# Moving first copies, one ReLU, two squares and one softmax scaling to other engines or later slots in a TensorE-bound kernel

## The chip, the cores and the metric

The kernel runs on one core of one Trainium2 chip. The metric is the device time of one execution in microseconds, lower is better. A ratio below is the mean time of one kernel's fast executions over the mean of the other's in the same rounds, so it is not quite the ratio of the medians that stand beside it.

Engine names in the profile: PE is TensorE (matmul), PEld its weight load, ACT ScalarE, DVE VectorE, POOL GpSimd, SP the engine that only issues DMA (SyncE).

## The reference, cut to what matters

A dynamic convolution over time (7 taps, weights by a softmax per position and head) feeds a feed-forward layer with a squared ReLU.

```python
w = exp(weight_gen - max); w = w / (sum(w) + 1e-09)          # 8 x 4096 x 8 heads x 7 taps
x = einsum('bshk,bskhg->bshg', w, x_unf)                      # causal window of 7
h = np.maximum(x.reshape(32768, 192) @ w_in, 0.0)             # 192 -> 2048
out = (h * h @ w_out).astype(np.float32)                      # 2048 -> 192
```

## The kernel before

Tokens go in blocks: two of 512, then blocks of 1024. A *block* j is: bands (VectorE spreads softmax weights over a mask), `st_conv` (the convolution as banded matmuls into PSUM, then a copy to `y`), *units* `u` (12 or 6 matmuls into a PSUM tile `h`; ReLU on ScalarE to `t`; square on VectorE to `g`), and *output groups* `M` (half of the 2048 rows of `g` times `w_out`). The output groups of a block run while the next block's units run.

```python
ps_h = ctx.enter_context(tc.tile_pool(name="ps_h", bufs=3, space=bass.MemoryType.PSUM))
ps_o = ctx.enter_context(tc.tile_pool(name="ps_o", bufs=1, space=bass.MemoryType.PSUM))
...
def st_conv(j):
    ...                                   # matmuls into the tiles yps (tag "h": the same 3 buffers)
    for n, yp in enumerate(yps):
        k0, k1 = n * per, min((n + 1) * per, NK)
        nc.scalar.copy(out=y[:, k0:k1, 0:th],
                       in_=yp[:, 0 : (k1 - k0) * th].rearrange("p (k c) -> p k c", c=th))

def st_unit(j, u):
    ...                                   # 12 (or 6) matmuls into h
    nc.scalar.activation(out=t1, in_=h, func=ActF.Relu)
    nc.vector.tensor_tensor(out=g, in0=t1, in1=t1, op=AluOp.mult)
```

The order on every engine is the order of the program, and a string per block spells it: `E` exponential (ScalarE), `S` sum, reciprocal and scaling of a softmax piece (VectorE), after the last piece of a part the row moves (DMA, alternately issued by SP and GpSimd), `B` bands, `C` the next block's convolution followed by an x load issued by GpSimd, `X` a cast of x on VectorE, `L` the load of a softmax part (DMA, issued by SP), `u` a unit, `M` an output group. A digit is the number of the part or block.

```python
plans = {
    0: "B1 X1 u u u E1 S1 u C u u u u",
    1: "L3 u u B2 M E2 B3 u M E2 u u S2 u M u C u S2 M",
    ...
    3: "L5 L6 M S3 u u u M u u u u M u M B6 E4 u u u M M B7 u u S4 u E4 M u C M u",
}
```

The first `M` of block 1 (M1 below) reads units 0 to 3 of block 0, the second (M2) reads units 4 to 7, unit 4 first.

The softmax here doesn't subtract the row's maximum and nothing guards it: scores larger than these inputs give would overflow.

## Time and profile before

| | before |
|---|---|
| median, 4 executions | 747.93 us (747.69 to 749.93) |
| profiled span | 746.6 us, granted clock 1.000 |
| busy | TensorE 99%, ScalarE 84%, VectorE 83%, GpSimd 12% |
| chain that ended last | TensorE 94% |

The prediction shows the lines and reads them.

### The profile page before, as it was taken

The page shows a single profiled execution, that of the slowest core. Times are in us where ns is not written, and L with a number is a line of the kernel's source. Part 1 is how long each engine was busy: PE and PEld are TensorE (multiplying, and loading weights), DVE is VectorE, ACT ScalarE, POOL GpSimd, SP SyncE. Part 2 cuts the span into 40 slices and gives each one's busy share as a digit, 9 for nine tenths or more (in the row PEclk, how much of TensorE's full clock was granted, in tenths as well). Part 3 has the DMA queues.
Part 4 walks back from the last instruction along what each step waited for, and adds up shares of the span by engine and source line. Part 5 has one row for each costly group of instructions (what it writes and reads, how often), then busy time and mean ns, then how long its engine had stood idle before and what let it go on. Part 6 is the DMA issues. An engine that isn't in the chain of part 4 may idle for free.

```text
span 746.6 us, 33289 instructions
## 1 busy us (share of the span) xinstructions
PE 739.0 (99%) x15106; PEld 556.5 (75%) x15106; DVE 621.8 (83%) x1001; ACT 624.7 (84%) x755; POOL 88.8 (12%) x130
## 2 busy tenths in 40 slices
PE   8999999999999999999999999999999999999998
PEld 4767877877777777777777777787777777777787
DVE  5999998998889888888889888898888987677853
ACT  5998788888888888888888888888888888888874
POOL 7321220101101100011000110001100011001000
PEclk9999999999999999999999999999999999999999
DMA  8654454436554234644245542365441354441312
GB/s 223 112 106 109 80 101 85 100 70 139 94 118 79 75 57 80 140 79 73 45 74 139 102 65 53 51 139 108 59 80 48 57 108 80 60 73 51 51 46 65
DMA packets 122169, 64.81 MB, mean 87 GB/s; under 512 B 83849, under 2 KB 118636, under 8 KB 121516
## 3 DMA queue, kind: packets, MB, share of 16 engines
q1 hardware_dynamic: 77708, 45.66, 22.4%
q0 software_dynamic: 44176, 16.93, 20.5%
q8 instruction: 118, 1.93, 1.1%
q14 instruction: 23, 0.19, 0.1%
q10 hardware_dynamic: 144, 0.10, 0.0%
HBM read 48.61 MB, written 28.70 MB: 104 GB/s over the span
## 4 chain that ended last, share of the span: by engine, by line
PE 94%; DVE 2%; issue 1%; DMA 1%; ACT 1%; POOL 0%; DVEq 0%; ACTq 0%
PE o L475 45%; PE h L441 43%; PE yp L416 6%; DVE g L453 1%; DVE bd L348 1%; DMA wr<-v_first 0%; DMA wg<-in_weight_gen_dram 0%; POOL wr L330 0%; ACT t L450 0%; DVE v_first L239 0%; ACT ex L217 0%; DVE ssum L224 0%; DVE rcp L231 0%; DVE o_sb L491 0%; ACT y L427 0%
## 5 line engine op out<-in xcount | busy, mean ns | idle before, releaser
L450 ACT ACTIVATE t<-h 128x1024 f16<-128x1024 f32 x512 | 496.7, 1026 | 65.6 <-PE h L441 65.3
L453 DVE TENSOR_TENSOR g<-t 128x1024 f16<-128x1024 f16 x512 | 334.3, 687 | 100.5 <-ACT t L450 97.8
L475 PEld LDWEIGHTS <-g 64*128 64x128 f16 (+1 forms) x8032 | 352.3, 94 | 55.0 <-issue 4.8
L475 PE MATMUL o<-w_o,g 64*128 64x192 f16 (+1 forms) x8032 | 385.3, 243 | 0.9 <-DVE o_sb L491 0.6
L441 PE MATMUL h<-y,w_i 64*128 64x512 f16 (+1 forms) x3168 | 379.7, 370 | 2.2 <-ACT t L450 0.9
L441 PEld LDWEIGHTS <-w_i 64*128 64x128 f16 x3168 | 162.6, 94 | 117.2 <-issue 5.2
L348 DVE TENSOR_TENSOR bd<-wr,mask 128x4160 f16<-128x4160 f16 (+3 forms) x89 | 149.3, 1701 | 4.0 <-DMA wr<-v_first 4.0
L300 POOL DMA_DIRECT2D xt<-in_x_dram x62 | 51.2, 830 | 446.7 <-PE yp L416 423.7
L489 ACT COPY o_sb<-o 128x384 f32<-128x384 f32 x129 | 62.2, 482 | 33.8 <-PE o L475 33.8
L491 DVE TENSOR_TENSOR o_sb<-o,o_sb 128x384 f32<-128x384 f32 x123 | 68.2, 555 | 8.4 <-ACT o_sb L489 5.6
L427 ACT CAST y<-yp 128x1024 f16<-128x1024 f32 (+1 forms) x64 | 48.1, 803 | 14.5 <-PE yp L416 14.5
L416 PE MATMUL yp<-bd,xt 128*32 128x104 f16 (+8 forms) x3864 | 51.7, 208 | 0.3 <-DVE bd L348 0.2
L416 PEld LDWEIGHTS <-xt 128*32 128x32 f16 (+3 forms) x3864 | 46.2, 92 | 6.7 <-issue 6.2
L239 DVE TENSOR_TENSOR v_big<-ex,rcp 128x112 f16<-128x112 f32 (+1 forms) x136 | 27.3, 263 | 1.8 <-DMA vd<-v_big 0.6
L217 ACT ACTIVATE ex<-wg 128x448 f32<-128x448 f32 (+2 forms) x44 | 27.2, 618 | 1.8 <-DMA wg<-in_weight_gen_dram 1.8
L224 DVE TENSOR_REDUCE ssum<-ex 128x64 f32<-128x448 f32 (+2 forms) x44 | 26.1, 594 | 2.5 <-ACT ex L217 2.3
L231 DVE RECIPROCAL rcp<-ssum 128x64 f32<-128x64 f32 (+2 forms) x44 | 23.7, 539 | 1.5
L290 POOL DMA_DIRECT2D xt<-in_x_dram x7 | 3.8, 549 | 135.8 <-PE yp L416 135.8
L330 POOL DMA_DIRECT2D wr<-v_first x31 | 16.8, 561 | 16.3 <-DVE v_first L239 16.1
L539 PE MATMUL wp<-warm 128*128 128x512 f16 x39 | 11.4, 459 | 1.3 <-DVE warm L531 1.3
L539 PEld LDWEIGHTS <-warm 128*128 128x128 f16 x39 | 4.3, 114 | 7.6 <-issue 3.5
L239 DVE TENSOR_TENSOR v_first<-ex,rcp 128x112 f16<-128x112 f32 (+1 forms) x48 | 9.1, 255 | 0.3
(24 smaller groups left out, 28.2 us busy)
## 6 DMA issues: line engine op xcount, KB each, us to landing
out_dram<-o_sb SPq DMA_DIRECT2D x63, 384.0 KB, 3.0
xt<-in_x_dram POOLq DMA_DIRECT2D x42, 240.0 KB, 5.9
wg<-in_weight_gen_dram SPq DMA_DIRECT2D x4, 1064.0 KB, 8.3
xt<-in_x_dram POOLq DMA_DIRECT2D x20, 192.0 KB, 5.6
wr<-vd SPq DMA_DIRECT2D x38, 80.0 KB, 3.6
vd<-v_big SPq DMA_DIRECT2D x5, 512.0 KB, 5.5
wg<-in_weight_gen_dram SPq DMA_DIRECT2D x5, 392.0 KB
wg<-in_weight_gen_dram SPq DMA_DIRECT2D x3, 616.0 KB, 4.1
```

Of the source, the lines that this page charges most:

```text
L217: nc.scalar.activation(out=self.ex[:, lo:hi].rearrange("p r g k e -> p (r g) k e"), in_=self.wg[:, lo:hi].rearrange("p r (g e) k -> p (r g ...
L239: eng.tensor_tensor(out=bass.AP(tensor=v.tensor, offset=v.offset + lo * H * SL + lo % SL * 2 + g * SL * 2, ap=[list(v.ap[0]), [H * SL + 2, ...
L300: eng.dma_start(out=dst[:, first:last], in_=ap)
L348: nc.vector.tensor_tensor(out=bd_t[j][:, H * lo : H * (lo + len(tiles) * n)].rearrange("p (g m c) -> p g m c", g=shape[1], c=2 * SL), in0= ...
L416: nc.tensor.matmul(out=yps[k // per][p0 : p0 + m, col + a : col + b], lhsT=x_t[s][:, i, 32 * q : 32 * q + m], rhs=bd[:, h // 2, h % 2, a - ...
L427: nc.scalar.copy(out=y[:, k0:k1, 0:th], in_=yp[:, 0 : (k1 - k0) * th].rearrange("p (k c) -> p k c", c=th),)
L441: nc.tensor.matmul(out=h[:, half, jj * th : (jj + 1) * th], lhsT=w_in_chunk(u * per + jj, slot, half), rhs=y_t[j][r0 : r0 + RT, k, 0:th], ...
L450: nc.scalar.activation(out=t1, in_=h, func=ActF.Relu)
L453: nc.vector.tensor_tensor(out=g, in0=t1, in1=t1, op=AluOp.mult)
L475: nc.tensor.matmul(out=oo[:, cc * Dm : (cc + 1) * Dm], lhsT=g[r0 : r0 + n, cc * P : (cc + 1) * P], rhs=w_o[r0 : r0 + n, fc, :], start=(fc ...
L489: nc.scalar.copy(out=o_sb, in_=o[0][:, c])
L491: nc.vector.tensor_tensor(out=o_sb, in0=o[1][:, c], in1=o_sb, op=AluOp.add)
```

## The change

Its intent: in block 0 TensorE waits for ScalarE's ReLUs and for the copy of the first `y`, and at 78 us for a PSUM add that stands behind softmax work on VectorE. So the copy is split over two engines, one ReLU goes to VectorE, VectorE is relieved of two squares by the nearly idle GpSimd, and the softmax scaling at 78 us goes to a later slot.

```diff
 # st_conv
-            nc.scalar.copy(out=y[:, k0:k1, 0:th], in_=yp[...])
+            copies = ((k0, k1, nc.scalar.copy),)
+            if j == 0:
+                copies = ((0, 1, nc.scalar.copy),) + tuple(
+                    (k, k + 1, nc.vector.tensor_copy) for k in range(1, NK))
+            for a, b, copy in copies: copy(out=y[:, a:b, 0:th], in_=yp[...])
 # st_unit
-        nc.scalar.activation(out=t1, in_=h, func=ActF.Relu)
+        if relu_dve: nc.vector.tensor_scalar_max(out=t1, in0=h, scalar1=0.0)
+        else:        nc.scalar.activation(out=t1, in_=h, func=ActF.Relu)
-        nc.vector.tensor_tensor(out=g, in0=t1, in1=t1, op=AluOp.mult)
+        (nc.gpsimd if pool else nc.vector).tensor_tensor(out=g, in0=t1, in1=t1, op=AluOp.mult)
 # the order: v = ReLU on VectorE and square on GpSimd, w = square on GpSimd
-            0: "B1 X1 u u u E1 S1 u C u u u u",
+            0: "B1 X1 u u u E1 v S1 C w u u u",
-            3: "... M M B7 u u S4 u E4 M u C M u",
+            3: "... M M B7 u u u M u M C S4 u",
 # softmax pieces in block 4 (block, unit): fifth part 0 -> 1, seventh part 1 -> 2
-            (1, 0): ((3, 15), (4, 0)),          (1, 2): ((4, 1), (5, 1), (5, 15)),
+            (1, 0): ((3, 15), (4, 1)),          (1, 2): ((4, 2), (5, 1), (5, 15)),
 # bands in block 4 at units 7 and 9 instead of 5 and 9
-            us = {6: (7, 9)}.get(j, ...)
+            us = {4: (7, 9), 6: (7, 9)}.get(j, ...)
```

Left out here: the entry that puts the exponential of a piece at unit 2 before unit 1. In block 3 the new string also drops the second `E4`, which then comes in block 4, and puts the `C` behind the last `M`.

## The prediction

> **What bounds the kernel now.** I read the page's busy row and its chain first, then the timeline of TensorE over the start (11 to 38 us) and around 78 us, where the chain leaves TensorE, and last the timelines of VectorE and GpSimd over the same start, because the change moves work between those queues.
>
> ```profile
> PE 739.0 (99%) x15106; PEld 556.5 (75%) x15106; DVE 621.8 (83%) x1001; ACT 624.7 (84%) x755; POOL 88.8 (12%) x130
> ...
> PE 94%; DVE 2%; issue 1%; DMA 1%; ACT 1%; POOL 0%; DVEq 0%; ACTq 0%
> ```
>
> TensorE is busy 99% of the span and carries 94% of the chain. Its matmuls are the same after the change, so the change can only win back, or add, time in which TensorE stands still. Relieving ScalarE or VectorE is worth nothing by itself. TensorE's timeline (start, length, line, idle time before it and who ended it):
>
> ```profile
> 15.55 2.80 PE L441 MATMUL h<-y,w_i 64*128 64x256 f16 x48 [0.89 <-ACT y L427]
> 18.41 0.91 PE L416 MATMUL yp<-bd,xt 128*32 128x104 f16 x72
> 19.32 0.83 PE L441 MATMUL h<-y,w_i 64*128 64x256 f16 x12
> 21.05 4.28 PE L441 MATMUL h<-y,w_i 64*128 64x256 f16 x60 [0.90 <-ACT t L450]
> 25.26 1.50 PE L475 MATMUL o<-w_o,g 128*128 128x192 f16 x16
> 26.69 0.83 PE L441 MATMUL h<-y,w_i 64*128 64x256 f16 x12
> 27.45 1.49 PE L475 MATMUL o<-w_o,g 128*128 128x192 f16 x16
> ...
> 77.57 0.24 PE L475 MATMUL o<-w_o,g 64*128 64x192 f16 x1
> 78.43 1.48 PE L475 MATMUL o<-w_o,g 64*128 64x192 f16 x31 [0.62 <-DVE o_sb L491]
> 79.68 0.66 PE L441 MATMUL h<-y,w_i 64*128 64x512 f16 x4
> ```
>
> A unit here is 12 matmuls; one costs about 0.69 us (elsewhere in this timeline 36 of them take from 28.88 to the next start at 30.95). So there are three places to win: 0.89 us before the first unit, which waits for the copy of y; the six units from 19.32 to 25.26 (one at 19.32, five from 21.05), which need 6 x 0.69 = 4.1 us but take 5.9, since each waits for one of three PSUM buffers that ScalarE empties (1.8 us); and one stop of about 0.8 us at 78 us (a group of 32 output matmuls normally takes 1.33 us to the next start; here 79.68 - 77.57 = 2.11).
>
> VectorE and GpSimd in the same start:
>
> ```profile
> 14.89 2.36 DVE L348 TENSOR_TENSOR bd<-wr,mask 128x3328 f16<-128x3328 f16 x2 [0.73 <-DMA wr<-v_first]
> 17.17 0.65 DVE L314 CAST xt<-x_st 128x960 f16<-128x960 f32 x1
> 20.12 0.97 DVE L224 TENSOR_REDUCE ssum<-ex 128x112 f32<-128x784 f32 x1
> 21.12 0.85 DVE L231 RECIPROCAL rcp<-ssum 128x112 f32<-128x112 f32 x1
> 22.01 1.45 DVE L239 TENSOR_TENSOR v_first<-ex,rcp 128x112 f16<-128x112 f32 x8
> ...
> 23.76 2.74 POOL L330 DMA_DIRECT2D wr<-v_first  x5 [4.22 <-DVE v_first L239]
> 26.45 0.63 POOL L294 DMA_DIRECT2D xt<-in_x_dram  x1
> 27.00 0.84 POOL L300 DMA_DIRECT2D xt<-in_x_dram  x1
> ```
>
> Here the reader is to see GpSimd's queue: after VectorE's scaling (step S1) it issues five row moves, then the x load that goes with the next convolution (step C), 4.1 us of issuing in all. These come in program order.
>
> **What the Trainium skill says.** (1) "GPSIMD Engine Reference", 3.1 Elementwise: a two-input tensor_tensor costs about 2.6 cycles an element, 4497 ns for 2048 fp32. Half of that is my estimate for one square of 1024: 2.25 us. GpSimd runs none in this trace; VectorE's same square takes 0.687 us. (2) "SBUF — State Buffer", Who interferes with whom: a VectorE instruction with two SBUF inputs and a GpSimd instruction that reads SBUF exclude each other for a whole instruction. Squares, scalings and bands are such; reduce, reciprocal and PSUM reads are not. No run yet shows it. (3) "TensorE: Matmul & The Clock Gate", table at its head: GpSimd's queue is strictly first in, first out. The trace agrees: row moves, then x load, at 23.76, 26.45, 27.00. (4) Same page, Part 1: the array falls to half clock after an idle window of about 3.4 us. The trace shows a granted clock of 1.000 throughout, but no idle that long.
>
> **The change, part by part.**
>
> *First y.* One ScalarE copy of 768 columns (0.80 us) becomes 256 on ScalarE and twice 256 on VectorE. ScalarE's copies take 0.59, 0.80, 1.01 us at 512, 768, 1024, so 0.38 at 256. For VectorE I interpolate between its scaling (112 elements, 0.27 us) and its PSUM add (384 elements, 0.555 us): 1.05 ns an element, so 0.42 us for 256, the second starting 0.34 after the first. All start near 14.7: done at 15.08, 15.14, 15.48. The first unit can begin at 15.15, but its third slot needs the last copy; it ends near 16.0 instead of 16.24. Gain 0.2 to 0.3 us there, and VectorE's bands start at 15.4 instead of 14.89.
>
> *ReLU of unit 3.* VectorE: 0.555 + 640 x 1.05 ns = 1.23 us. Its queue before that: bands 15.4 to 17.7, cast to 18.3, three squares (about 0.63 each) to 20.2, so ReLU to 21.4. ScalarE finished it at 21.0 before. So the unit that waits for this buffer starts at 21.45 instead of 21.05. But ScalarE, without 0.93 us of work, is now ahead, and the later short waits (0.24 each, three times) go: 21.45, 22.1, 22.8, 23.5, 24.25, and the first output group (M1) at about 24.95 instead of 25.26. Gain at that point: 0.3 us.
>
> *Squares of units 3 and 4 on GpSimd.* Unit 3: 21.5 to 23.75, in time for M1. S1 on VectorE: reduce to 22.35, reciprocal to 23.2, scaling held by the port until 23.75, done at 25.2 (23.46 before). GpSimd then: start lag 0.3, row moves 2.74 to 28.2, x load 1.39 to 29.6, and only now the square of unit 4, because in the plan it stands behind S1 and C: to 31.9, or 32.9 if it must let the first band of 2.3 us end at about 30.6. The second output group (M2) reads unit 4 first. It is due at 24.95 + 1.43 + 0.76 = 27.15 and TensorE takes its work in order. So TensorE stands about 4.8 us. M2 starts near 32 instead of 27.45: loss 4.5 us, with the 0.3 gained above already in it.
>
> *Fifth softmax part.* Its scaling (1.97 us of VectorE from reduce to scale) stood before a PSUM add that frees the output banks. It now stands after the last output group and after the convolution, so the add comes at once and 1.5 + 0.65 us of matmuls lie between it and the next group. The stop at 78 us goes: gain 2.11 - 1.33 = 0.78 us. The bands moved from slot 5 to slot 7 in block 4 lie beside TensorE's work; nothing.
>
> Sum: +4.5 - 0.8 = +3.7 us, and 0.3 for a chance of about one in eight that the array loses clock in the stop (some 2.5 us then). 748.1 + 4.0 = 752.1.
>
> **Rivals.** *A, no stop at M2:* the first copy, the ReLU and the moved scaling give 0.3 to 2.5 us and the kernel comes to 745 to 747.5. For it: the aim of the change, and the 1.8 us of buffer waits. Against: GpSimd issues 4.1 us of DMA between the end of S1 and unit 4's square, and S1 can't end before about 24.6 even with no port held, so the square can't begin before 29. That is after 27.15 at any speed of GpSimd. It takes an order in GpSimd's queue other than the program's. I give it 0.13. *B, no exclusion at the port:* S1 ends at 24.65, square 29.05 to 31.3, M2 +3.9, total about 751.3. *C, the port starves GpSimd:* VectorE runs its bands (4.6 us) and a square without a gap, GpSimd gets in near 33.8, M2 +8.7, and an idle beyond 6 us costs the clock as well: 756 to 759. For it: band follows band with no gap from 27.84 to 32.43 before. Against: the third band needs rows that land about 1.7 us later now, which opens the port at 30.6.
>
> **Range and chances.** B to the main case spans 751 to 753; half of C's tail and A's near end give 748 to 756.5 for eight in ten. Repeats of before lie 2.2 us apart, 0.3%, so noise adds little. 2% is 15 us; nothing on the list reaches that: faster 0.01, same 0.97, slower 0.02.
>
> **What would show it.** TensorE's timeline after: an idle of 4 to 6 us before the second x16 group of output matmuls, ended by GpSimd's square; GpSimd's timeline with that square behind five row moves and an x load; unit 3's square near 2.2 us; a first unit near 15.15; no idle near 78 us ended by the PSUM add. The forecast falls if GpSimd does that square before the row moves, or if M2 starts before 29 us.

## The result

The changed kernel took 754.41 us (752.73 to 755.22, 4 executions) against 747.93, a ratio of 1.0078 with a 95% interval of 1.0052 to 1.0104: slower by about 6 us. That is within the predicted range (748 to 756.5), above the 751 to 753 that the prediction spans between its rival B and its main case, and inside the band of 2% called the same.

The page's busy row and chain of the changed kernel:

```profile
PE 740.0 (98%) x15106; PEld 564.2 (75%) x15106; DVE 625.6 (83%) x1002; ACT 623.8 (83%) x754; POOL 93.4 (12%) x132
...
PE 93%; DVE 4%; DMA 1%; POOL 1%; issue 1%; ACT 0%; DVEq 0%; ACTq 0%
```

The number of matmuls is the same and the busy time of every engine nearly so. Totals don't show where 6 us went; the chain shows a little more of VectorE and GpSimd. TensorE's timeline over the start does show it (start, length, line, idle time before it and what ended it):

```profile
16.94 2.91 PE L448 MATMUL h<-y,w_i 64*128 64x256 f16 x47 [0.19 <-DVE y L434]
20.51 0.91 PE L416 MATMUL yp<-bd,xt 128*32 128x104 f16 x72 [0.66 <-DVE xt L314]
...
23.44 3.69 PE L448 MATMUL h<-y,w_i 64*128 64x256 f16 x60 [1.26 <-DVE t L458]
27.06 1.50 PE L485 MATMUL o<-w_o,g 128*128 128x192 f16 x16
28.48 0.83 PE L448 MATMUL h<-y,w_i 64*128 64x256 f16 x12
33.08 2.74 PE L485 MATMUL o<-w_o,g 128*128 128x192 f16 x16 [3.77 <-POOL g L463]
```

M1 is the group at 27.06, M2 the one at 33.08. M2 stands idle 3.77 us until GpSimd has made a square. And the same 16 matmuls then take 2.74 us, where M1 took 1.50. The view of stretches tells why (start and end, length, busy time of TensorE, its loads, VectorE, ScalarE and GpSimd, then the granted clock):

```profile
33.00:36.00 3.00, 2.92 (x20) 2.44 (x22) 3.00 (x2) 1.17 (x2) 0.02 (x1) 0.51 0.59 81
```

The clock granted over these 3 us is 0.51. GpSimd's timeline shows what the square had to wait for:

```profile
23.47 1.89 POOL L463 TENSOR_TENSOR g<-t 128x1024 f16<-128x1024 f16 x1 [3.50 <-DVE t L458]
26.97 2.79 POOL L330 DMA_DIRECT2D wr<-v_first  x5 [1.61 <-DVE v_first L239]
29.68 0.65 POOL L294 DMA_DIRECT2D xt<-in_x_dram  x1
30.23 0.87 POOL L300 DMA_DIRECT2D xt<-in_x_dram  x1
31.01 2.01 POOL L463 TENSOR_TENSOR g<-t 128x1024 f16<-128x1024 f16 x1
```

Unit 4's ReLU had ended at 23.24. Its square (the last line) starts at 31.01, behind five row moves and two parts of an x load, as the program orders. VectorE's timeline over the same time:

```profile
16.47 0.76 DVE L434 CAST y<-yp 128x256 f16<-128x256 f32 x2 [0.94 <-ACT y L434]
...
22.18 1.21 DVE L458 TENSOR_SCALAR t<-h 128x1024 f16<-128x1024 f32 x1
...
30.15 7.33 DVE L348 TENSOR_TENSOR bd<-wr,mask 128x4160 f16<-128x4160 f16 x3 [0.43 <-DMA wr<-v_first]
```

and the same three bands in the kernel before:

```profile
27.84 4.59 DVE L348 TENSOR_TENSOR bd<-wr,mask 128x4160 f16<-128x4160 f16 x3
```

VectorE's copies of the first `y` start when ScalarE's has ended (16.43), not beside it. The three bands take 7.33 us instead of 4.59: the first alone takes 5.07 instead of 2.32, while GpSimd's second square runs. At the place of the old stop at 78 us there is none any more, but a new one stands further on:

```profile
95.01 0.24 PE L485 MATMUL o<-w_o,g 64*128 64x192 f16 x1
95.66 1.48 PE L485 MATMUL o<-w_o,g 64*128 64x192 f16 x31 [0.41 <-DVE o_sb L501]
```

To compare runs I count from the start of the last matmul of the first convolution. Everything before it is the same program, yet it came between 14.08 and 15.82 us over the traces (14.46 before, 15.82 in the changed kernel), with the time that the first row moves took to land (4.60 us on the chain of the changed kernel, 2.76 on that of e5 below). Start times on that clock, in us:

| | M1 | M2 | unit after M2 | convolution 2 | convolution 5 | end |
|---|---|---|---|---|---|---|
| before | 10.81 | 13.00 | 14.42 | 18.68 | 84.33 | 732.11 |
| changed | 11.24 | 17.26 | 19.93 | 24.27 | 89.74 | 737.50 |
| difference | +0.43 | +4.26 | +5.51 | +5.59 | +5.41 | +5.39 |

So 0.43 us are lost before M1, 3.83 more waiting for M2, 1.25 more in M2 at half clock and 0.08 up to convolution 2; 0.18 come back by convolution 5, and after it the two stay level. That sums to 5.4 of the 6.7 us between the two profiled spans; the other 1.36 us is the start (15.82 - 14.46), which is not the change's.

### The profile page after: what moved, and what is told of

Same layout as the page of the kernel before. It is cut to its first block, busy times and chain, and to the rows that moved or that the text cites. A ratio compares the mean times of both kernels' runs of the same rounds, so it can differ in the third digit from the quotient of the medians.

```text
span 753.3 us, 33290 instructions
## 1 busy us (share of the span) xinstructions
PE 740.0 (98%) x15106; PEld 564.2 (75%) x15106; DVE 625.6 (83%) x1002; ACT 623.8 (83%) x754; POOL 93.4 (12%) x132
## 4 chain that ended last, share of the span: by engine, by line
PE 93%; DVE 4%; DMA 1%; POOL 1%; issue 1%; ACT 0%; DVEq 0%; ACTq 0%
PE o L485 45%; PE h L448 42%; PE yp L416 6%; DVE bd L348 1%; DVE g L463 1%; DMA wr<-v_first 1%; DVE v_first L239 0%; DMA wg<-in_weight_gen_dram 0%; DVE ssum L224 0%; DVE rcp L231 0%; POOL wr L330 0%; POOL g L463 0%; DVE o_sb L501 0%; DVE t L458 0%; ACT t L460 0%
## 5 line engine op out<-in xcount | busy, mean ns | idle before, releaser
L448 PEld LDWEIGHTS <-w_i 64*128 64x128 f16 x3168 | 168.4, 94 | 112.2 <-issue 5.2
L348 DVE TENSOR_TENSOR bd<-wr,mask 128x4160 f16<-128x4160 f16 (+3 forms) x89 | 152.1, 1732 | 5.2 <-DMA wr<-v_first 5.2
```

The costliest lines, as they stand in the source:

```text
L348: nc.vector.tensor_tensor(out=bd_t[j][:, H * lo : H * (lo + len(tiles) * n)].rearrange("p (g m c) -> p g m c", g=shape[1], c=2 * SL), in0= ...
L448: nc.tensor.matmul(out=h[:, half, jj * th : (jj + 1) * th], lhsT=w_in_chunk(u * per + jj, slot, half), rhs=y_t[j][r0 : r0 + RT, k, 0:th], ...
```

## The experiments

Theory: M2 waits because unit 4's square stands behind GpSimd's DMA issuing, and the idle then costs the clock. Rivals: the shared port between GpSimd and VectorE costs the time; GpSimd is too slow for a square wherever it stands; the ReLU or the copies cost it. Each run was timed in five rounds beside the kernel before; the twelve kernels went out in three calls, each to another chip, and the median of before was 749.26, 748.51 and 748.19 us in them. So ratios are to be compared, not medians across calls. The expectations count from the 747.93 us of the first measurement. "Clock" times in the text are on the clock of the table above.

**e1: unit 4's square back on VectorE** (on the changed kernel)

```diff
-            0: "B1 X1 u u u E1 v S1 C w u u u",
+            0: "B1 X1 u u u E1 v S1 C u u u u",
```

> The changed kernel with the square of unit 4 back on VectorE; all else of the change stays. Theory (the second output group waits for that square, which stands in GpSimd's queue behind row moves and x load): the idle of 3.8 us before that group goes, and with it the half clock after it (1.25 us), so some 5.2 us less than the changed kernel, 748 to 749.3 us. Rival 1 (the loss is VectorE held up by GpSimd's squares at the shared port, or the ReLU and copies it was given): unit 3's square, the ReLU and the copies are still there, so at least half of the loss stays, above 751 us.

Measured: 749.26 us against 749.26, ratio 1.0000 (0.9988 to 1.0012). The whole loss is gone with this one square. TensorE's timeline: M2 comes without a wait and at full speed:

```profile
28.68 1.49 PE L485 MATMUL o<-w_o,g 128*128 128x192 f16 x16
```

M1 is at 11.24, exactly where the changed kernel has it, M2 at 13.43 instead of 17.26. Rival 1 falls as far as it means the ReLU, the copies and the other square: they are all still there. What unit 4's square itself does at the port left with it. The trace of the changed kernel bounds that: the square took 2.01 us there and 1.89 for unit 3, so the port can have added some 0.1 us to M2's wait; e2 and e7 test the rest.

**e2: unit 4 ahead of the scaling and the convolution, its square still on GpSimd** (on the changed kernel)

```diff
-            0: "B1 X1 u u u E1 v S1 C w u u u",
+            0: "B1 X1 u u u E1 v w S1 C u u u",
```

> The changed kernel with unit 4 moved ahead of the scaling S1 and the convolution, so that its square stands in GpSimd's queue before the row moves and the x load; it still runs on GpSimd. Theory (queue order): the second output group waits less than 0.5 us; but two squares in a row hold up the scaling, so rows and bands come some 2 us later and the next convolution waits 1 to 2.5 us: 749 to 751 us. Rival 2 (GpSimd is simply too slow for a square wherever it stands): the group still waits 2 us or more for GpSimd, 752 us or more.

Measured: 752.79 us, ratio 1.0041 (1.0023 to 1.0058). TensorE's timeline up to 37 us:

```profile
27.65 1.49 PE L485 MATMUL o<-w_o,g 128*128 128x192 f16 x16
...
34.23 0.22 PE L416 MATMUL yp<-bd,xt 128*32 128x104 f16 x2 [0.82 <-DVE bd L348]
35.94 1.34 PE L416 MATMUL yp<-bd,xt 128*32 128x104 f16 x55 [1.48 <-DVE bd L348]
```

M2 follows M1 after 2.19 us, as in the kernel before, so a square on GpSimd does no harm to M2 if it stands before the DMA issues; rival 2 falls on that. But the loss is at the upper edge of the 1.1 to 3.1 us that I expected (3.1 us by the ratio, 3.5 by the medians). Two squares in a row held up the scaling (3.19 us for its eight instructions, 1.45 before), the rows landed from 28.7 to 32.7 us, and convolution 2 stood idle twice, 0.82 and 1.48 us, for the bands. The granted clock fell to 0.67 in the stretch from 35 to 40 us. Of six executions, three had a mean clock of 1.000 (750.96 to 752.18 us) and three 0.998 (753.39 to 754.46). The mechanism was as expected, but I had not counted on the clock, and why some rows took 3 us to land, others 2, stays open.

**e3: the wait filled with dummy matmuls** (on the changed kernel; 14 matmuls on zeros into one of the three `h` buffers, before M2)

```diff
-            1: "L3 u u B2 M E2 B3 u M E2 ...",
+            1: "L3 u u B2 M E2 B3 u W M E2 ...",     # W: 14 matmuls of 512 columns
```

> The changed kernel with 14 dummy matmuls of 512 columns (some 3 us) in TensorE's queue just before the second output group, which has to wait anyway. Theory (the idle drops the granted clock and the group after it runs slow): the group starts at the same place but takes 1.5 instead of 2.7 us, granted clock 1.00 throughout; the time falls by about 1.2 us to 753.2. Rival (the slow group is slow for another reason, or the trace's modelled ends mislead): the time stays at 754.4 and the group takes 2.7 us.

Measured: 752.67 us, ratio 1.0040 (1.0028 to 1.0052). TensorE's timeline:

```profile
27.65 3.19 PE L715 MATMUL fill_t<-warm 128*128 128x512 f16 x14
31.49 1.50 PE L485 MATMUL o<-w_o,g 128*128 128x192 f16 x16 [0.65 <-POOL g L463]
```

M2 starts no earlier (17.40 against 17.26 on the common clock) and still waits for GpSimd, but now takes 1.50 us, and all five executions have a clock of 1.000. Up to convolution 5 this kernel is 1.28 us ahead of the changed one (88.46 against 89.74). The half clock is a cost of its own: 1.25 us of the loss. By the ratios the gain is 2.8 us (1.0078 to 1.0040), more than the 1.2 expected and than the trace shows; what the rest is stays open.

**e4: only the moved scaling of the fifth part** (on the kernel before)

```diff
-            3: "... B7 u u S4 u E4 M u C M u",
+            3: "... B7 u u u M u M C S4 u",
-            (1, 0): ((3, 15), (4, 0)),   (1, 2): ((4, 1), (5, 1), (5, 15)),
+            (1, 0): ((3, 15), (4, 1)),   (1, 2): ((4, 2), (5, 1), (5, 15)),
-            us = {6: (7, 9)}.get(j, ...)
+            us = {4: (7, 9), 6: (7, 9)}.get(j, ...)
```

> The kernel before with only the scaling of the fifth softmax part moved. What the trace of the changed kernel shows: the stop at 78 us goes (0.75 us), a new one of 0.55 us comes in the next block where a PSUM add now stands behind two softmax pieces; net -0.2 us, 747.7. Rival (the prediction's step): -0.78 us, 747.15, no new stop.

Measured: 748.63 us, ratio 0.9993 (0.9980 to 1.0005). From M1 to convolution 5 it takes 73.36 us, the kernel before 73.52: 0.16 us won, as the trace of the changed kernel had shown. The new stop is there, ended by the PSUM add as before:

```profile
88.58 1.48 PE L475 MATMUL o<-w_o,g 64*128 64x192 f16 x31 [0.47 <-DVE o_sb L491]
```

**e5: only the first y by two engines** (on the kernel before; the diff of `st_conv` above)

> The kernel before with only the first y copied by two engines. What the trace of the changed kernel suggests: VectorE's copies do not run beside ScalarE's but after it, so the first unit starts earlier and then stops for the second copy; units 0 to 3 gain nothing (0.1 us lost), bands and cast on VectorE come 0.8 us later and the convolution after them waits: +0.2 to +0.6 us in all, 748.1 to 748.5. Rival (the prediction's step): the first four units end 0.2 to 0.3 us earlier, 747.6 to 747.9.

Measured: 748.88 us, ratio 1.0007 (0.9994 to 1.0020). M1 comes 0.16 us later than before (10.97), convolution 5 0.19 us later. The prediction's gain is not there. That there is a loss is not shown: the times don't resolve it, and in e4 and e10, whose program up to M1 is that of the kernel before, M1 came at 11.01 and 10.83 and convolution 1 at 4.48 and 4.71 (3.95 before, 4.50 here), because the rows for the bands landed later.

**e6: only unit 3's ReLU on VectorE**, its square on VectorE too (on the kernel before; `r` is a unit of that kind)

```diff
-            0: "B1 X1 u u u E1 S1 u C u u u u",
+            0: "B1 X1 u u u E1 r S1 C u u u u",
```

> The kernel before with only unit 3's ReLU on VectorE; its square stays on VectorE. Theory (VectorE has no room here): ReLU of 1.2 us ends near where ScalarE's did, the first output group gains up to 0.3 us, but scaling, rows and bands come 1.2 us later and the next convolution waits about 0.5 to 0.8 us: 748.0 to 748.5. Rival (relieving ScalarE pays): -0.3 us or more, 747.6 or less.

Measured: 750.03 us against 748.51, ratio 1.0017 (1.0005 to 1.0029). M1, M2 and the start of convolution 2 come 0.24 us earlier, as predicted for a relieved ScalarE. Then that convolution stops after two matmuls:

```profile
33.62 1.56 PE L416 MATMUL yp<-bd,xt 128*32 128x104 f16 x118 [0.79 <-DMA xt<-in_x_dram]
```

The x load is issued by GpSimd behind the row moves, which wait for the scaling, which the ReLU pushed back. By convolution 3 the kernel is 0.77 us behind. The times show 1.3 us (0.4 to 2.2), more than the 0.1 to 0.6 expected. I had expected bands to end that wait; it was the load.

**e7: only unit 4's square on GpSimd** (on the kernel before)

```diff
-            0: "B1 X1 u u u E1 S1 u C u u u u",
+            0: "B1 X1 u u u E1 S1 u C w u u u",
```

> The kernel before with only unit 4's square on GpSimd, behind row moves and x load as in the change. Theory (queue order): GpSimd's queue is free at 27.8, square to about 29.9, so the second output group waits about 2.4 us[...]: +2.4 us, 750.3. Rival 1 (the port): the band that runs beside the square is stretched and the loss is 4 us or more. Rival (the aim of the change): VectorE relieved by one square, no wait, 748 or less.

Measured: 752.51 us, ratio 1.0048 (1.0035 to 1.0062). TensorE, then GpSimd, then VectorE:

```profile
30.39 1.49 PE L478 MATMUL o<-w_o,g 128*128 128x192 f16 x16 [2.33 <-POOL g L456]
```

```profile
28.34 1.99 POOL L456 TENSOR_TENSOR g<-t 128x1024 f16<-128x1024 f16 x1
```

```profile
27.77 3.12 DVE L456 TENSOR_TENSOR g<-t 128x1024 f16<-128x1024 f16 x1 [0.22 <-ACT t L453]
```

M2 comes 2.42 us later than before (15.42), and that stays to convolution 5 (+2.46): the expected size, from the expected place, with none of the change's other parts. In time the loss is larger, about 3.6 us, where the expectation held no cost in clock. The two executions with a clock of 0.999 and 1.000, the profiled one among them, took 751.35 and 751.03 us; the three with 0.997 or 0.998 took 752.51 to 753.96. So the idle of 2.33 us seems to cost clock in some executions; that is read from means, and not shown: only one execution was traced, and its granted clock stayed at 1.00 from 25 to 40 us. The third fence is the port: a VectorE square that began 0.57 us before GpSimd's took 3.12 us, where one takes 0.687. It is not what M2 waited for.

**e8: the moved scaling, and the next heavy piece moved too** (e4 with one number more)

```diff
-            (1, 2): ((4, 2), (5, 1), (5, 15)),
+            (1, 2): ((4, 5), (5, 1), (5, 15)),
```

> The kernel before with the fifth part's scaling moved as in the change, and the first piece of the seventh part (which the change put one unit after it) moved four units later, to just behind a PSUM add. Theory (the new stop comes from that add standing behind two softmax pieces in VectorE's queue): both stops go, -0.75 us, 747.2. Rival (the stop comes from squares or from the bands): a stop of 0.4 us or more stays in that block, 747.7.

Measured: 749.67 us, ratio 1.0015 (1.0000 to 1.0029). My theory fell: the stop moved one round on and grew.

```profile
94.60 1.48 PE L475 MATMUL o<-w_o,g 64*128 64x192 f16 x31 [1.14 <-DVE o_sb L491]
```

Now that PSUM add stood behind the moved piece and two bands.

**e9: the first y in two PSUM tiles** (on the kernel before; slots 0 and 1 in one tile, copied by ScalarE, slot 2 in another, copied by VectorE)

```diff
-        per = 1024 // th
+        per = 2 if j == 0 else 1024 // th
...
-            nc.scalar.copy(
+            copy = nc.vector.tensor_copy if j == 0 and n == 1 else nc.scalar.copy
+            copy(
```

> The kernel before with the first y in two PSUM tiles instead of one: ScalarE copies slots 0 and 1 (512 columns) from the first, VectorE slot 2 from the second, at the same time. Theory (in the change VectorE's copies waited for ScalarE's because both read one PSUM tile): VectorE's copy starts within 0.1 us of ScalarE's; the first unit starts 0.2 us earlier (0.85 to 0.9 us after the convolution's last matmul instead of 1.09) with no second stop, first output group 0.1 to 0.2 us earlier; the time cannot show that: 0 to -0.3 us. Rival (VectorE and ScalarE can't read PSUM side by side there): VectorE's copy again begins after ScalarE's, a second stop of 0.4 us in the first unit.

Measured: 748.35 us against 748.19, ratio 1.0001 (0.9987 to 1.0014). ScalarE's copy and VectorE's:

```profile
15.04 0.59 ACT L428 CAST y<-yp 128x512 f16<-128x512 f32 x1 [2.09 <-PE yp L416]
```

```profile
15.10 0.42 DVE L428 CAST y<-yp 128x256 f16<-128x256 f32 x1 [0.55 <-PE yp L416]
```

They start 0.06 us apart, both released by TensorE. In the changed kernel VectorE's first copy waited for a semaphore that ScalarE's copy raises; here it waits for TensorE's, as ScalarE's copy does. So the wait was one that the program makes, and VectorE and ScalarE do copy side by side. What makes the program wait is not separated: in the changed kernel the two copies share a tile and also one of its two halves of 512 columns (slots 0 and 1 lie in it), here they share neither. The first unit starts 0.84 us after the convolution's last matmul instead of 1.09, and M1 comes 0.25 us earlier, which convolution 5 still has (84.10 against 84.33). The times don't resolve a quarter of a microsecond.

**e10: the moved scaling with every heavy piece behind its own PSUM add** (e8 with the bands of block 4 later)

```diff
-            us = {4: (7, 9), 6: (7, 9)}.get(j, ...)
+            us = {4: (9, 12), 6: (7, 9)}.get(j, ...)
```

> The kernel before with the fifth part's scaling moved as in the change, the first piece of the seventh part four units later, and the two bands of that block at units 9 and 12 instead of 7 and 9, so that each heavy piece of VectorE stands right behind a PSUM add, one between two adds. Theory (a stop comes wherever two heavy pieces stand between two PSUM adds, because the later add is late): no stop over 0.3 us from 70 to 105 us, -0.75 us against before, 747.4 to 748.2 where before is 748.5. Rival (VectorE has too much work in that stretch however it is ordered): a stop of 0.5 us or more remains.

Measured: 748.26 us, ratio 1.0002 (0.9990 to 1.0015). No PSUM add stops TensorE between 70 and 97 us any more, and convolution 5 starts 0.83 us earlier than before. Then the later bands stop that very convolution:

```profile
98.34 1.85 PE L416 MATMUL yp<-bd,xt 128*32 128x104 f16 x118 [0.38 <-DVE bd L348]
```

Two bands in a row stop it: 0.61 and 0.30 us lie from one matmul to the next, and right after it 0.31 us in an output group, ended by a PSUM add. By convolution 6 the kernel is 0.39 us behind before (107.28 against 106.89). The rival has it so far: in three orders of the same pieces (e4, e8, e10) VectorE's lag always reached TensorE somewhere in this stretch. That no order avoids it is not shown.

**e11: e9 and e10 together**

> The two repairs above together, and nothing of the ReLU or the squares on GpSimd. If both hold, -0.9 us against before, a ratio of 0.9988, just outside of what the interval resolves; never above before.

Measured: 747.79 us against 748.19, ratio 0.9999 (0.9987 to 1.0012). Convolution 5 is 1.17 us ahead (83.16), convolution 6 is 0.06 us behind (106.95), for the reason that e10 shows. Not slower, and not faster.

**e12: e11 with unit 3's ReLU on VectorE and its square on GpSimd**

> The run above with unit 3's ReLU on VectorE and its square on GpSimd as in the change, the square of unit 4 on VectorE. Theory (GpSimd's first square is free because it runs beside reduce and reciprocal, but the ReLU pushes scaling, rows and bands back): first output group 0.2 to 0.3 us earlier than the run above, the convolution after it stops for 0.3 to 0.8 us, in sum 0 to +0.5 us against the run above. Rival (with the square taken off, VectorE has room for the ReLU): no stop in that convolution, another -0.3 us.

Measured: 748.58 us, ratio 1.0007 (0.9995 to 1.0020). M1 comes at 10.13, 0.42 us ahead of e11 and 0.68 us ahead of before; convolution 2 then stops 0.38 us from one matmul to the next, ended by the x load as in e6, and by convolution 6 (106.88) it stands level with before (106.89). GpSimd's first square is harmless where it is: it ran beside the sum and the reciprocal.

No kernel here beats the one before by more than its interval. The best are e4 (0.6 us under before by its median) and e11 (0.4 us), both within the noise.

## Why the prediction was right or wrong

The direction and the place were forecast, and the size within the range: 752.1 us predicted, 754.41 measured. The cause is the one named, unit 4's square behind GpSimd's row moves and x load. e1 shows that the loss goes with it, e7 that it comes with it alone, e2 that M2's wait goes when unit 4 stands ahead of them. Point by point:

- *Squares on GpSimd: right.* Predicted: M2 4.5 us later than before; measured 4.26. Row moves and x load were taken from the trace at 2.74 and 1.39 us; they measured 2.79 and about 1.4. The square's estimate of 2.25 us was too long: 1.89 and 2.01. That it came so close is in part luck, as two errors cancelled: unit 3's ReLU ended 0.63 us later than predicted (7.57 on the clock for 6.94), and the scaling was not held the predicted 0.55 us at the port, so that it ended at 10.86 for 10.74.
- *The clock: right in kind, mis-sized.* The failed step is "0.3 for a chance of about one in eight that the array loses clock in the stop". It came in all four executions of the changed kernel (mean clock 0.995 to 0.998) and cost 1.25 us in the traced one; e3 isolates it. With idles of 3.8 us it was no chance, and e2 shows it after shorter ones. Neither the one in eight nor rival C's "beyond 6 us" was worked out from a trace.
- *First y: wrong.* The failed step is "All start near 14.7": VectorE's copies began after ScalarE's, so the first unit stopped a second time, bands and cast began 0.88 us later on the clock than before (0.5 predicted for the bands) and convolution 1 waited 0.66 us for the cast. The cast also took 1.05 us instead of 0.65, which stays open. e5 alone: M1 0.16 us later, within the scatter of the traces, in place of the 0.2 to 0.3 predicted gain. e9 shows that two tiles give the predicted gain.
- *ReLU: right on its own.* 1.23 us predicted, 1.21 measured; M1 0.24 us earlier in e6 against 0.3 predicted. In the changed kernel the ReLU stood in VectorE's queue behind the late bands and cast, and the unit that waits for its buffer stopped 1.26 us (0.90 before): M1 was 0.43 later, where I had it 0.3 earlier. That 0.7 us is no part of the miss at M2, which waits for GpSimd: a later TensorE only waits less.
- *Fifth softmax part: wrong.* The failed step is "gain 2.11 - 1.33 = 0.78 us". The stop at 78 us did go, but one of 0.65 us from one matmul to the next came in block 4: net 0.16 us in e4. I looked at what the add at 78 us stood behind, and not at what the next one would stand behind once the pieces had moved on.
- *The port: the other side.* I feared that VectorE would hold GpSimd off its second square until a band ended, or longer (rival C). The band was held instead, for 2.75 us. It cost TensorE nothing in the changed kernel, as M2 was late anyway.

Together: the clock (+0.95 over what I had put in), the softmax part (+0.6), 0.08 between M2 and convolution 2, less 0.24 for M2. That gives the traced 5.4 us in place of my 4.0.

## What to carry to other kernels

Before giving work to an idle engine, list what its in-order queue holds between the moment the work could start and the moment its result is read: GpSimd was busy 12% of the time and still was 4 us late, because the work stood behind DMA issues that waited for something else. Removing one stop of the bounding engine is worth only the distance to the next: here three reorderings of VectorE's pieces each moved the stop, and none kept more than 0.2 us of the 0.8 that it cost. And an idle of a few microseconds on TensorE can cost a second time, by a lower granted clock after it.

## What the Trainium skill lacked or had wrong

- "SBUF — State Buffer", Who interferes with whom: it says that the shared port is an exclusive lock and that the order of issue decides who blocks. Here VectorE's instruction with two SBUF inputs came first by its recorded start and still was the one stretched: a band begun 0.86 us before GpSimd's square took 5.07 instead of 2.32 us, and a square begun 0.57 us before took 3.12 instead of 0.687. GpSimd's square took 1.99 and 2.01 us there and 1.89 (unit 3's) beside instructions that don't share the port, and TensorE started 0.06 us after its recorded end. VectorE's two ended 2.20 and 0.56 us after GpSimd's, nearly their whole unhindered length, as if they had done almost nothing before. Whether GpSimd holds the port from before its recorded start, which would save the page's rule, is not shown; the recorded starts alone don't say who blocks.
- "GPSIMD Engine Reference", 3.1 Elementwise: its measured figure is for 2048 fp32 elements. Half of it, an estimate, is 2.25 us; 1024 fp16 elements took 1.89 to 2.01 us here.
- "TensorE: Matmul & The Clock Gate", Part 1: it speaks of an idle window of about 3.4 us. In e2 two idles of 0.82 and 1.48 us, with two matmuls between, came before a granted clock of 0.67 over 5 us; in e7 three of five executions with an idle near 2.3 us had a mean clock of 0.997 or 0.998. An idle of 3.8 us cost it in four of four.
